# Attention in one block a two pairs of heads instead of two, from the tenth two pairs on

## The chip, the cores and the metric

One core of a Trainium2 chip. The metric is the device time of one execution in microseconds (us); of the kernel before there are three runs, with a median of 1277.4. Engines are named as in the profile: PE is TensorE (PEld its weight loads), DVE VectorE, ACT ScalarE, POOL GpSimd, SP the queue of SyncE, which issues most DMAs.

## The reference, cut to what matters

Eight batch elements, 12 heads, 448 rows, head dimension 64; all in float32.

```python
def rmsnorm(x, g): return x / sqrt(mean(x * x, -1) + 1e-06) * g
scores = 1 / sqrt(64) * rmsnorm(q, g_q) @ rmsnorm(k, g_k).T
attn   = exp(scores - max) / (sum + 1e-09)
x      = (attn @ v), heads side by side                      # (8, 448, 768)
h      = relu(x.T @ w_tok1) @ w_tok2;   u = x + h.T          # token mixing, 256 wide
out    = u + relu(u @ w_ch1) @ w_ch2                         # channel mixing, 1536 wide
```

## The kernel before, in words

**What is computed where.** The kernel works on one batch element's mixing while it computes the attention of the next element between the mixing's matmuls. Heads go in pairs (p, 48 in all, 6 an element), and attention goes in steps of two pairs (t, 24 in all, 3 an element), so that the four heads of a step fill the four 64x64 quarters of TensorE. For key block k of 64 rows (7 of them, `NK`), `score(t, k)` (line 451) does the score matmuls of four heads into two PSUM tiles and two exponentials on ScalarE into an SBUF tile `e`; `values(pair, k)` (521) multiplies `e` with v and accumulates in one PSUM tile `o_ps` a pair; `group_sums` (495) adds the `e` tiles up on VectorE; `row_sums` (540) adds over rows with matmuls of ones into `d_ps`; `denominators` (546) has three kinds of part: `begin` transposes `d_ps` on VectorE and takes the reciprocal, `raw` copies `o_ps` to SBUF on ScalarE, `end` spreads the reciprocal by another transpose and multiplies, both on VectorE. A matmul of float32 stands in the trace as two instructions, so a score step is x8.

**Norms of a later step.** q and k of pairs n and n+1 are loaded by SP (`loads`, 1405, 8 DMAs a pair for pairs from 12 on), squared on ScalarE (`square`, 1432), reduced on VectorE (`reduce`, 1446); then `roots` (1510) gives the parts `fold` (four ScalarE copies), `guess` (VectorE) and three `newton` steps, each of four instructions (GpSimd for pairs from 20 on); `scale` (1501) multiplies on VectorE, and `turn_qk` (423) transposes on VectorE and, for q (i = 0), multiplies by g on ScalarE.

**Mixing of an element b.** `tok1` (843) in halves h = 0 and 1 of the channels (for the second half the rows left over go first, four 64-row matmuls a half, line 854), relu on ScalarE (`tok1_out`); `tok2` (886), six products, each evacuated by VectorE (line 894), and `moving_sums` (902). Then 21 channel units `ch1` (997; 3 groups of seven products, i = 0 to 6, 12 matmul instructions each), of which i = 0 and i = 4 are evacuated by a ScalarE copy (after i = 4 two additions on GpSimd follow), the others by VectorE; then 30 halves of products with w_ch2 (`ch2`, 1065; 15 products f in two halves x, 8 matmul instructions each), whose evacuation is written out in `C_STEPS`, that of f = 0 being a ScalarE copy. Element 1 has 12 halves `plain_2` (1051) instead. All their products use `m_tile`, of which there are two buffers (`ps_M`, line 140); score and d tiles share four (`ps_S`, 138), `o_ps` has two (139). x of an element is transposed from the attention's output by `trans_x` (814) on VectorE, sent to DRAM and loaded again (`send_x`, `load_x`), by SP or, for the second half of element 2, by GpSimd.

**Order.** Every engine but SP runs in the order in which the Python program calls things (`manual_schedule`, line 88). The order is written out by hand: lists of items (cost, function), joined by `merge` (66), which takes from the list that is least far on by its costs, and by `place` (638), which puts blocks at given places among the mixing units and deals the small items that follow a block evenly over the units up to the next block. `run` (170) calls the items, and `later` (162) calls a function when the sum of the costs has passed a time. The `load_units` (925) prefetch keeps up to seven weight units ahead on SP.

**Attention of t = 9 on.** Up to t = 8 attention comes in four `att_step`s (657) a t. From t = `BIG` = 9 on, `big_step` gives two blocks a t. The first block has the scores of key blocks 0 and 1, the last values (key blocks 4, 5 and 6) and row sums of the t before, and score 2; the second has scores 3 and 4, values 0 to 3, scores 5 and 6. The first square of the next pairs is ahead of a first block, the first reduce and second square inside it, the scales and two of the four transposes right after a second block. The first block of t = 9 stands in element 1; elements 2 to 6 have six blocks each, ahead of mixing units 0, 6, 11, 17, 23 and 31 (`BLOCKS`, 1240), counted from the element's first channel unit; the last of element 6 holds only the end of t = 23.

There is a second arm of the program (`shifted`) for inputs of large scale, which these inputs don't take.

Of the kernel before, what the change touches and what calls it, by code (L numbers as in the profile page):

```python
# [83 lines left out]
def whole(ctx, tc, shifted, pre, q, k, v, g_q, g_k, moe_w_tok1, moe_w_tok2, moe_w_ch1, moe_w_ch2, out):  # L84
# [13 lines left out]
    NPAIR = H // 2  # L98
# [15 lines left out]
    NM = S // P  # L114
    assert S - NM * P == D and NM == NS - 1 and NJ == 2

    UNITS = 8
    WCOLS = 512

# [287 lines left out]

    def load_v(p):
        b, hs = heads(p)
        st["v", p] = vt = pre.v_0 if p == 0 else st["v45"][:, p - 4, :] if p in (4, 5) else pre.v_t[p % 3]  # L410
        for a in range(2):
            nc.sync.dma_start(
                out=vt[rows_of(p, a)].rearrange("r (k d) -> r k d", d=D),
                in_=v[b, hs][a].rearrange("(k r) d -> r k d", r=D))
# [36 lines left out]
    def score(t, k):  # L451

        e = st["e", t, k] = e_tile(t >= BIG and ((t - BIG) * NK + k) % 5 == 4)
        pss = [s_tile("s_ps") for i in range(2)]
        for i in range(2):
            qkT = st["qkT", 2 * t + i]
            for a in range(2):
                h = slice(a * D, a * D + D)
                nc.tensor.matmul(  # L459
                    out=pss[i][rows_of(i, a), 0:S], lhsT=qkT[h, 1, k * D:(k + 1) * D], rhs=qkT[h, 0, :],  # L460
                    start=True, stop=True)
        for i in range(2):
            nc.scalar.activation(out=e[:, i, :], in_=pss[i][:, 0:S], func=AF.Exp)  # L463
# [82 lines left out]
    def denominators(ps):  # L546

        def begin(p):
            b, j = divmod(p, NPAIR)
            if j == 0:  # L550
                st["uT", b] = uT_pool.tile([P, NC, S], F32, name="uT")
            ps = st.pop(("d", p))

            dt = rd_pool.tile([P, S], F32, name="dt", tag="rd")
            if shifted:
                nc.vector.tensor_scalar(dt[:], ps[:, 0:S], 1e-9, None, ALU.add)
                src = dt[:]
            else:

                src = ps[:, 0:S]  # L560
            nc.vector.transpose(out=dt[:], in_=src)
            st["rc", p] = rc = pre.nt_pool.tile([P, NB], F32, name="rc")
            nc.vector.reciprocal(out=rc[:], in_=dt[:].rearrange("p (n c) -> p n c", c=32)[:, :, 0])

        def raw(p):

            b, j = divmod(p, NPAIR)
            to = st["uT", b][:, j, :]
            nc.scalar.copy(out=to, in_=st["o", p][:, 0:S])
            st["o", p] = to  # L570

        def end(p):
            b, j = divmod(p, NPAIR)
            rd = rd_pool.tile([P, S], F32, name="rd", tag="rd")
            nc.vector.transpose(
                out=rd[:].rearrange("p (n c) -> p n c", c=32),
                in_=st.pop(("rc", p))[:].unsqueeze(2).to_broadcast([P, NB, 32]))
            nc.vector.tensor_tensor(out=st["uT", b][:, j, :], in0=st.pop(("o", p))[:, 0:S], in1=rd[:], op=ALU.mult)

        parts = [lambda p=p: begin(p) for p in ps]  # L580
        if ps[0] < NPAIR:
# [4 lines left out]
    BIG = NPAIR + NPAIR // 2  # L586

    def big_step(t, second):

        p, n = 2 * t, 2 * t + 2  # L590
        pair, last, live, more = (p, p + 1), (p - 2, p - 1), p < NP, 2 * t + 2 < NP
        item = lambda fn, *a, c=0.4: (c, lambda: fn(*a))
        loads = lambda j: [(0.3, fn) for fn in pre.loads(j, st, nc.sync, nc.sync)] if j < NP else []

        def first_block():
            if live:
                score(t, 0)
                score(t, 1)
# [21 lines left out]
        if not second:  # L620
            squares = [item(fn, i, st) for i in (n, n + 1) for fn in (pre.square, pre.reduce)] if more else []
            ahead, beside = (squares[:1], squares[3:]) if t > BIG else ([], [])
            between = [item(group_sums, t, k) for k in (1, 2) if live]
            ends, roots = ([(0.4, fn) for fn in fns] for fns in (denominators(last), pre.roots(n, st) if more else []))
            if t == BIG:
                return ahead, (5.4, first_block), beside, between + ends + [
                    item(load_v, i, c=0.0) for i in pair] + squares + roots
            between += roots[:1] + ends[:2] + roots[1:2]
            between += [it for both in zip(ends[2:], roots[2:4]) for it in both] if more else ends[2:]
            between += roots[4:] + [item(load_v, i, c=0.0) for i in pair if live]  # L630
            return ahead, (5.4, first_block), beside, between
        beside = [item(scale, n), item(scale, n + 1), item(turn_qk, n, 1), item(turn_qk, n, 0)] if more else []
        beside += [item(group_sums, t, k) for k in (3, 4)]
        between = [item(turn_qk, n + 1, 1), item(turn_qk, n + 1, 0)] + loads(n + 2) if more else []
        between += [item(group_sums, t, k) for k in (5, 6)] + loads(n + 3)
        return [], (6.2, second_block), beside, between

    def place(units, blocks, at):

        res, i, rest = [], 0, []  # L640
        for j, (ahead, block, beside, between) in list(zip(at, blocks)) + [(len(units), ([], None, [], []))]:
            n, done = j - i, 0
            for m in range(n):
                if m == n - 1 and block:
                    res += ahead
                res.append(units[i + m])
                upto = -(-len(rest) * (m + 1) // n)
                res += rest[done:upto]
                done = upto
            if not n:  # L650
                res += rest + ahead
            i, rest = j, between
            if block:
                res += [block] + beside
        return res

    def att_step(g):
# [95 lines left out]
            items.append((0.0, lambda: load_v(p + 1)))  # L753
        if live and s == 1 and 5 < p + 2 < NP:
            items.append((0.0, lambda: load_v(p + 2)))
        js = []
        if live and s == 0:
            js = [n, n + 1] if pre.plain(p) else [n + 1]
# [493 lines left out]
    left, (some, sums) = [], sum_items()  # L1252
    for b in range(B):
        early, double = middle_items(b)
        if b == 0:
# [21 lines left out]
        att = []  # L1277
# [301 lines left out]
```

## Time and profile before

| what | value |
|---|---|
| runs, us | 1277.4, 1273.76, 1279.42 (median 1277.4) |
| profiled execution, us | 1277.84, its span 1275.4 |
| granted TensorE clock, mean | 0.997 |
| score matmuls (line 459, qkT) | x1260, 144.2 us busy |
| value matmuls (line 532, e) | x1148, 129.8 us busy |
| exponentials (line 463, e) | x294, 554 ns each |
| row additions (line 500, es and e) | x90, 1139 ns each |
| normalising multiply (line 1507, 128x896) | x36, 1276 ns each |
| transposes of q and k (line 436) | x72, 618 ns each |

The span runs from the first to the last instruction of the profiled execution; 2.4 us of its time lie around it. The chain of waits starts from the last instruction and goes back at each step to what released it, or to the instruction before it on its engine; its lines give start, length, engine, tile and line. A timeline line gives start, length, engine, line, operation, out<-in with shapes, and in brackets how long the engine had been idle and what released it.

### The profile page before, as it was taken

How to read it: one execution, taken by the hardware profiler on the slowest of the kernel's cores; microseconds unless marked ns; L12 is line 12 of the kernel's file. 1: busy time of each engine (PE TensorE's matmuls, PEld its weight loads, DVE VectorE, ACT ScalarE, POOL GpSimd, SP SyncE). 2: the span in 40 equal slices, each digit the busy share in tenths (PEclk: the TensorE clock that was granted, in tenths of full speed). 3: DMA queues.
4: the chain of work that ended last, by engine and by line, in shares of the span. 5: the costliest groups of instructions: out<-in, count | busy, mean ns of one | idle time of the engine just before them, and what ended most of it. 6: DMA issues, size and time to landing. Idle time of an engine off the chain costs nothing.

```text
span 1275.4 us, 20051 instructions
## 1 busy us (share of the span) xinstructions
PE 1252.2 (98%) x7250; PEld 891.1 (70%) x7250; DVE 796.5 (62%) x1241; ACT 393.9 (31%) x785; POOL 407.0 (32%) x646
## 2 busy tenths in 40 slices
PE   6999999999999999999999999999999999999998
PEld 3444444457645488796778777885787867797998
DVE  6988879756663455855577356765558456554243
ACT  6664433124330134402442044312343024300210
POOL 2310651044994822231223112241122322131222
PEclk9999999999999899999999999999999999999999
DMA  9666687899889686695758767685866864376654
GB/s 204 158 172 174 197 226 188 197 263 253 224 216 260 139 200 162 146 244 110 169 146 188 181 147 181 147 223 121 181 159 150 231 136 139 116 199 145 192 174 105
DMA packets 480272, 228.37 MB, mean 179 GB/s; under 512 B 362900, under 2 KB 440084, under 8 KB 480164
## 3 DMA queue, kind: packets, MB, share of 16 engines
q1 hardware_dynamic: 472626, 211.85, 67.7%
q0 software_dynamic: 4512, 14.46, 3.9%
q8 instruction: 59, 0.97, 0.3%
q10 hardware_dynamic: 3026, 0.69, 0.3%
q14 instruction: 49, 0.40, 0.1%
HBM read 184.26 MB, written 42.66 MB: 178 GB/s over the span
## 4 chain that ended last, share of the span: by engine, by line
PE 88%; DVE 4%; DMA 3%; SPq 1%; ACT 1%; issue 1%; DVEq 0%; ACTq 0%
PE m_ps L1009 26%; PE m_ps L1075 22%; PE s_ps L459 10%; PE o_ps L532 9%; PE m_ps L889 6%; PE m_ps L979 5%; PE m_ps L847 2%; PE t_ps L847 2%; PE m_ps L1058 1%; PE d_ps L512 1%; PE m_ps L512 1%; DMA raw<-wp 1%; DVE stage L383 1%; PE m_ps L854 1%; PE t_ps L433 1%
## 5 line engine op out<-in xcount | busy, mean ns | idle before, releaser
L1075 PE MATMUL m_ps<-hb,unit 128*128 128x224 f32 x1440 | 277.2, 354 | 0.0
L1075 PEld LDWEIGHTS m_ps<-hb,unit 128*128 128x128 f32 x1440 | 270.9, 190 | 8.8 <-issue 7.7
L1009 PE MATMUL m_ps<-tu,unit 128*128 128x224 f32 x1008 | 201.6, 355 | 1.3 <-ACT r L1019 1.3
L1009 PEld LDWEIGHTS m_ps<-tu,unit 128*128 128x128 f32 x1008 | 189.1, 190 | 15.0 <-issue 9.2
L463 ACT ACTIVATE e<-s_ps 128x448 f32<-128x448 f32 x294 | 138.6, 554 | 177.5 <-PE s_ps L459 168.9
L1009 PE MATMUL m_ps<-uT,unit 128*128 128x224 f32 x756 | 151.2, 354 | 0.8 <-DVE hb L1015 0.8
L1009 PEld LDWEIGHTS m_ps<-uT,unit 128*128 128x128 f32 x756 | 142.2, 190 | 7.9 <-issue 4.6
L459 PE MATMUL s_ps<-qkT 64*64 64x448 f32 x1260 | 144.2, 545 | 0.8 <-ACT x L829 0.8
L532 PE MATMUL o_ps<-e,v 64*64 64x448 f32 x1148 | 129.8, 538 | 0.0
L500 DVE TENSOR_TENSOR es<-es,e 128x896 f32<-128x896 f32 x90 | 102.5, 1139 | 13.4 <-ACT e L463 8.4
L1015 DVE TENSOR_TENSOR hb<-m_ps,r 128x448 f32<-128x448 f32 x63 | 39.1, 621 | 106.2 <-POOL r L1015 57.4
L1015 POOL TENSOR_TENSOR hb<-r,r 128x448 f32<-128x448 f32 x21 | 23.9, 1140 | 239.0 <-ACT r L1031 239.0
L459 PEld LDWEIGHTS s_ps<-qkT 64*64 64x64 f32 x1260 | 45.5, 132 | 69.5 <-issue 59.2
L532 PEld LDWEIGHTS o_ps<-e,v 64*64 64x64 f32 x1148 | 45.9, 133 | 61.9 <-issue 59.6
L1486 POOL TENSOR_TENSOR nt<-rs 128x56 f32<-128x56 f32 (+1 forms) x54 | 21.8, 403 | 201.4 <-DVE rs L1478 198.5
L1016 ACT ACTIVATE hb<-hb 128x448 f32<-128x448 f32 x84 | 48.4, 577 | 100.4 <-DVE hb L1015 77.4
L1090 POOL TENSOR_TENSOR uT<-uT,r 128x448 f32<-128x448 f32 x42 | 51.4, 1241 | 78.3 <-DVE r L1090 46.6
L889 PE MATMUL m_ps<-w_sb,h 128*128 128x448 f32 x192 | 75.2, 544 | 0.3 <-DVE uT L894 0.3
L324 POOL TENSOR_TENSOR raw<-raw 128x128 f32<-128x128 f32 x128 | 64.8, 527 | 21.8 <-DMA raw<-wp 17.3
L894 DVE TENSOR_TENSOR uT<-uT,m_ps 128x448 f32<-128x448 f32 x48 | 29.3, 614 | 65.9 <-PE m_ps L889 65.8
L1456 DVE TENSOR_REDUCE ms<-sq 128x28 f32<-128x896 f32 (+2 forms) x44 | 47.4, 1080 | 36.7 <-ACT sq L1443 29.6
L1015 DVE TENSOR_TENSOR r<-m_ps,r 128x448 f32<-128x448 f32 x42 | 26.1, 622 | 64.5 <-PE m_ps L1009 64.5
(153 smaller groups left out, 1626.9 us busy)
## 6 DMA issues: line engine op xcount, KB each, us to landing
unit<-ws SPq DMA_DIRECT2D x267, 384.0 KB, 4.2
raw<-in_moe_w_ch_dram SPq DMA_DIRECT2D x72, 256.0 KB, 3.5
v<-in_v_dram SPq DMA_DIRECT2D x96, 112.0 KB, 3.5
out_dram<-turned SPq DMA_DIRECT2D x182, 56.0 KB, 2.0
xs<-xt SPq DMA_DIRECT2D x52, 168.0 KB, 4.8
qk_t<-in_q_dram SPq DMA_DIRECT2D x144, 56.0 KB, 3.5
qk_t<-in_k_dram SPq DMA_DIRECT2D x144, 56.0 KB, 3.9
x<-xs SPq DMA_DIRECT2D x39, 192.0 KB, 4.0
```

The lines of the kernel that those rows point to most:

```text
L324: nc.gpsimd.tensor_tensor(out=at[o], in0=at[x], in1=at[y], op=ALU.add if op == "+" else ALU.subtract)
L459: nc.tensor.matmul(out=pss[i][rows_of(i, a), 0:S], lhsT=qkT[h, 1, k * D:(k + 1) * D], rhs=qkT[h, 0, :], start=True, stop=True)
L463: nc.scalar.activation(out=e[:, i, :], in_=pss[i][:, 0:S], func=AF.Exp)
L500: nc.vector.tensor_tensor(out=es[:], in0=(es if k > 1 else st["e", t, 0])[:], in1=st["e", t, k][:], op=ALU.add)
L532: nc.tensor.matmul(out=st["o", p][a * D:(a + 1) * D, 0:S], lhsT=vt[rows, k * D:(k + 1) * D], rhs=e[rows, :], **kw)
L847: nc.tensor.matmul(out=st["t1", h][jc][:, 0:HC], lhsT=w1_sb[:, c, jc * P:(jc + 1) * P], rhs=st["x", b, h][:, :, c, :], start=start and c = ...
L889: nc.tensor.matmul(out=ps[:, 0:S], lhsT=st["h1", jc][:, cc * P:(cc + 1) * P], rhs=w2_sb[:, jc].rearrange("p c r -> p (c r)"), start=(jc == ...
L979: nc.tensor.matmul(out=ps, lhsT=a[:, o + 2 * half, :], rhs=natural(half * KF + t) if wide else u[:, half * KC + t, :], start=(t == 0 and h ...
L1009: nc.tensor.matmul(out=ps[:, j * HS:(j + 1) * HS], lhsT=w[:, t, j, :], rhs=m, start=(t == 0), stop=(t == KC - 1))
L1015: add = lambda e, o, x, y: e.tensor_tensor(out=o, in0=x, in1=y, op=ALU.add)
L1075: nc.tensor.matmul(out=ps[:, x * HS:(x + 1) * HS], lhsT=st["w"][:, tile_at % 6, :], rhs=hb[:, X_SLOT[f], i, :], start=(i == 0), stop=(i == 3))
L1090: e.tensor_tensor(out=get(out), in0=get(x_), in1=get(y), op=ALU.add if op == "+" else ALU.subtract)
```

## The change

From t = 9 on, attention comes in one block a t. It holds scores 0 and 1 of t, values 5 and 6 and the row sums of the t before, then for that t `begin` and `raw` of both pairs (so `o_ps` is copied to SBUF by ScalarE, which was done for the first element only), then score 2, and from there value k-3, row addition k-1 and score k in turn for k = 3 to 6, and value 4. The last row addition follows the block. Elements 2 to 6 have three blocks each, ahead of mixing units 2, 15 and 31.

What follows a block is dealt out by `place` alone, in one row: the two `end`s, the v loads of the next t, the norms (two squares, two reduces, five root parts), the scales, transposes and loads; nothing of it is ahead of a block or inside one any more. After an element's third block only `end`s, v loads and the first two norm items stand; the rest of the norms (`behind`) is merged with the last mixing units and the second half of x, and the scales, transposes and loads (`carry`) are dealt over the next element's units from its `tok1` up to its first block. The whole norms of t = 10, which stood behind the block of t = 9 in element 1, go with that carry into element 2. The v tiles of pairs from 18 on use four buffers instead of three, and pair 19's load is moved to t = 8. In element 1, the list of attention items that `merge` joins with the mixing changes its costs: 5.4 for the first block and 6.0 for what follows it before, 11.3 and 1.2 after.

```diff
+    BIG = NPAIR + NPAIR // 2
...
     def load_v(p):
         b, hs = heads(p)
-        st["v", p] = vt = pre.v_0 if p == 0 else st["v45"][:, p - 4, :] if p in (4, 5) else pre.v_t[p % 3]
+        if p >= 2 * BIG and not shifted:
+            vt = (pre.v_0, pre.v_t[0])[p % 2] if p // 2 % 2 else pre.v_t[1 + p % 2]
+        else:
+            vt = pre.v_0 if p == 0 else st["v45"][:, p - 4, :] if p in (4, 5) else pre.v_t[p % 3]
+        st["v", p] = vt
...
-        if ps[0] < NPAIR:
+        if ps[0] < NPAIR or ps[0] >= 2 * BIG - 2 and not shifted:
             parts += [lambda p=p: raw(p) for p in ps]
...
-    def big_step(t, second):
+    def big_step(t):
...
+        ends = denominators(last)
-        def first_block():
+        def block():
             if live:
                 score(t, 0)
                 score(t, 1)
-            if more and t > BIG:
-                pre.reduce(n, st)
-                pre.square(n + 1, st)
-            for k in range(NK - 2 - (t > BIG), NK):
+            for k in (NK - 2, NK - 1):
                 values(last, k)
             row_sums(t - 1)
             for i in last:
                 st.pop(("v", i))
-            if live:
-                score(t, 2)
-
-        def second_block():
-            score(t, 3)
-            score(t, 4)
-            for k in range(4):
-                values(pair, k)
-            score(t, 5)
-            score(t, 6)
+            for part in ends[:4]:
+                part()
+            if not live:
+                return
+            group_sums(t, 1)
+            score(t, 2)
+            for k in range(3, NK):
+                values(pair, k - 3)
+                group_sums(t, k - 1)
+                score(t, k)
+            values(pair, NK - 3)
...
+        beside = [item(group_sums, t, NK - 1)] if live else []
+        ends_ = [(0.4, fn) for fn in ends[4:]]
+        if not more:
+            return (11.3 if live else 2.3, block), beside, ends_, [], []
+        norms = [item(fn, i, st) for i in (n, n + 1) for fn in (pre.square, pre.reduce)]
+        norms += [(0.4, fn) for fn in pre.roots(n, st)]
+        turned = [item(scale, n), item(scale, n + 1), item(turn_qk, n, 1), item(turn_qk, n, 0)] + loads(n + 2)
+        turned += [item(turn_qk, n + 1, 1), item(turn_qk, n + 1, 0)] + loads(n + 3)
+        values_in = [item(load_v, i, c=0.0) for i in (n, n + 1)]
+        return (11.3, block), beside, ends_ + values_in, norms, turned
...
-    BLOCKS = (0, 6, 11, 17, 23, 31)
+    BLOCKS = (2, 15, 31)
...
-                ahead, block, beside, between = big_step(BIG, False)
-                att = att[6:] + att_items(lo + 10, lo + per - 1) + ahead + [block] + beside + between
+                block, beside, ends_, norms, turned = big_step(BIG)
+                att = att[6:] + att_items(lo + 10, lo + per - 1) + [block] + beside + ends_
+                carry = norms + turned
         elif b + AHEAD < B:
             t = (b + AHEAD) * NPAIR // 2
-            blocks = [big_step(t + i // 2, i % 2) for i in range(1, NPAIR + 1)]
-            blocks[4][3].extend(x_items(b + 1, 0))
-            early = place(early, blocks, [near(early, at) for at in BLOCKS])
+            steps = [big_step(t + i) for i in range(1, NPAIR // 2 + 1)]
+            blocks = [(block, beside, ends_ + norms + turned) for block, beside, ends_, norms, turned in steps[:2]]
+            blocks[1][2].extend(x_items(b + 1, 0))
+            block, beside, ends_, norms, turned = steps[2]
+            blocks.append((block, beside, ends_ + norms[:2]))
+            early = place(early, blocks, [near(early, at) for at in BLOCKS], carry)
+            behind, carry = norms[2:], turned
...
-                last = merge(last, x_items(b + 1, 1))
+                last = merge(last, x_items(b + 1, 1) + behind)
```

More of the change, by code (lines that the diff above doesn't have):

```diff
@@ L585, in whole @@
     NG = 2 * NP
-    BIG = NPAIR + NPAIR // 2
-    def big_step(t, second):
+    assert BIG % 2
+    def big_step(t):
         p, n = 2 * t, 2 * t + 2
@@ L617, in second_block @@
+            values(pair, NK - 3)
             for i in pair:
                 st.pop(("qkT", i))
[L620 to L641, printed above, removed]
+        beside = [item(group_sums, t, NK - 1)] if live else []
@@ L642, in place @@
+        return (11.3, block), beside, ends_ + values_in, norms, turned
+    def place(units, blocks, at, rest):
+        res, i = [], 0
+        for j, (block, beside, between) in list(zip(at, blocks)) + [(len(units), (None, [], []))]:
             n, done = j - i, 0
             for m in range(n):
-                if m == n - 1 and block:
-                    res += ahead
                 res.append(units[i + m])
@@ L650, in place @@
             if not n:
-                res += rest + ahead
+                res += rest
             i, rest = j, between
@@ L755, in att_step @@
             items.append((0.0, lambda: load_v(p + 2)))
+            if t == BIG - 1 and not shifted:
+                items.append((0.0, lambda: load_v(p + 3)))
         js = []
@@ L1251, in whole @@
         att_items(0, 8) + merge(att_items(8, AHEAD * per + 1), x_items(0, 0)), weight_items(0, BEFORE)))
-    left, (some, sums) = [], sum_items()
+    left, carry, (some, sums) = [], [], sum_items()
     for b in range(B):
@@ L1276, in whole @@
         lo = (b + AHEAD) * per + 1
-        att = []
+        att, behind = [], []
         if b + AHEAD < B and (shifted or b < 2):
```

## The prediction

> **What bounds the kernel now.** I read the page first, then the chain of waits by stretches, then the engines' timelines where the chain leaves TensorE. The page:
>
> ```profile
> PE 1252.2 (98%) x7250; PEld 891.1 (70%) x7250; DVE 796.5 (62%) x1241; ACT 393.9 (31%) x785; POOL 407.0 (32%) x646
> PE 88%; DVE 4%; DMA 3%; SPq 1%; ACT 1%; issue 1%; DVEq 0%; ACTq 0%
> ```
>
> TensorE is busy nearly throughout and is 88% of the chain that ended last. The chain of waits from 440 us on (start, us, what) holds nothing but TensorE up to the last microseconds:
>
> ```profile
> 439.55 1.67 PE s_ps L459 x16
> 441.22 3.01 PE o_ps L532 x32
> 444.22 1.50 PE s_ps L459 x16
> 445.73 13.82 PE m_ps L1009 x72
> 459.54 1.66 PE s_ps L459 x16
> ...
> 502.12 9.28 PE m_ps L1009 x48
> ```
>
> So after 440 us no VectorE, ScalarE or DMA work costs anything; what can be saved is TensorE's own time, and any new wait is lost in full. Two prices are in these lines. Sixteen score matmuls take 1.50 inside a block but 1.67 at its start: 0.17 to enter. Channel matmuls: (13.82 - 9.28) / (72 - 48) = 0.189 each, and 72 x 0.189 = 13.62, so each stretch carries 0.20 for leaving a block. **A block costs 0.37 us** beyond its matmuls.
>
> Before 440 the chain has two holes. At the start of element 2, x comes late:
>
> ```profile
> 416.18 4.96 DMA x<-xs
> 421.14 0.14 issue
> 421.27 2.31 PE t_ps L854 x4
> 423.58 6.85 PE t_ps L847 x12
> ```
>
> The same two rows at the start of element 3:
>
> ```profile
> 573.79 0.65 PE t_ps L854 x4
> 574.44 4.07 PE t_ps L847 x12
> ```
>
> TensorE idled 2 us for x, then worked at about half speed for 8 us (the windows view grants 0.52 of the clock from 422 to 429). Against its matmuls' usual spacing, this hole costs 5.9. The other, at 328 to 332, is VectorE and ScalarE evacuating late while they normalise pairs 16 and 17:
>
> ```profile
> 323.85 2.53 DVE qk_t L1507 x2
> ...
> 328.07 0.56 ACT hb L1016
> ...
> 331.86 2.54 PE m_ps L1009 x12
> ```
>
> It costs 2.7 (TensorE's gaps in loading weights there are 1.2 and 1.65).
>
> The normalisation of the next two pairs, which the change moves, is a chain over four engines (timeline, 394 to 403; the last two lines from 589):
>
> ```profile
> 394.66 0.95 ACT L1443 ACTIVATE sq<-qk_t 128x896 f32<-128x896 f32 x1 [12.16 <-DMA qk_t<-in_k_dram]
> 395.64 1.09 DVE L1456 TENSOR_REDUCE ms<-sq 128x28 f32<-128x896 f32 x1 [6.87 <-ACT sq L1443]
> 396.76 1.01 ACT L1464 COPY half<-ms 32x56 f32<-32x56 f32 x4 [1.15 <-DVE ms L1456]
> ...
> 398.34 0.27 POOL L1486 TENSOR_TENSOR nt<-rs 128x56 f32<-128x56 f32 x1 [6.78 <-DVE rs L1478]
> ...
> 402.31 0.30 POOL L1489 TENSOR_TENSOR rs<-nt,rs 128x56 f32<-128x56 f32 x1
> ...
> 589.27 2.55 DVE L1507 TENSOR_TENSOR qk_t<-qk_t,rs 128x896 f32<-128x896 f32 x2
> 591.75 1.16 DVE L436 STREAM_TRANSPOSE qkT<-qk_t 128x448 f32<-128x448 f32 x2
> ```
>
> Second square to roots ready: 402.6 - 394.66 = **8.0**, of which GpSimd's three steps are 4.2. Then VectorE scales (2.55) and transposes (1.16).
>
> [...]
>
> **The change, part by part.** The sum is against the profiled execution, 1277.84 (span 1275.4).
>
> 1. **Fewer blocks.** Before: one block in element 1 and six in each of elements 2 to 6, 31. After: 16. Scores, values and row sums stay the same matmuls. 15 x 0.37 = **-5.5**; nothing hides it.
>
> 2. **Inside a block.** A score step, a value step and a row sum take 0.75 each on TensorE. Counting from the block's start, the row sums end at 0.17 + 5 x 0.75 = 3.92; the fourth score is due at 5.42 and needs their two PSUM tiles, which VectorE's two transposes free at 3.92 + 0.07 + 1.43 = 5.42 (1.43: two transposes with a reciprocal between, 541.10 to 542.53). The first values, due at 4.67, need the two new ScalarE copies (0.5 each, from 3.24): 4.3. Exponentials take 0.96 per 1.5 of TensorE. So it just fits; I take 16 x 0.06 = **+1.0** (0 to +5 if VectorE is behind when it enters). Row additions end 1.2 after the block, before the next unit's evacuation at 2.3.
>
> 3. **First gap of elements 2 to 5** (13 units, 35 items, dealt by `place`). From the block's end, a channel unit is 12 x 0.189 = 2.27. The second square is dealt after the unit with i = 4 (third in the gap), so on ScalarE it stands behind that unit's copy, which ends at 6.81 + 0.1 + 0.53 = 7.44. Chain 8.0: roots at 15.45. The unit with i = 0 (sixth in the gap) is followed on VectorE by scale, transpose, transpose: VectorE is bound till 15.45 + 2.55 + 1.16 = 19.2, and only then evacuates the seventh unit (0.6): 19.8. The ninth unit needs that PSUM buffer (two of them) at 8 x 2.27 = 18.16. Wait 1.65. Element 6 has no loads to deal, its items lie further apart, no wait. 4 x 1.65 = **+6.6** (0 to +10).
>
> 4. **Second gap of elements 2 to 5** (16 units, 38 items). GpSimd takes the Newton steps after the adds of the i = 4 unit: its end 9.08, copy 9.7, two adds (1.14 each) 12.05, Newton 16.3, scale 18.85, transposes 20.0, ScalarE's multiply (0.67) 20.7, and behind that, on ScalarE, the copy of the first w_ch2 product, 21.25. The third product needs its buffer at 6 x 2.27 + 4 x 1.51 = 19.67. Wait 1.6. 4 x 1.6 = **+6.4** (0 to +10).
>
> 5. **Third block.** Two norm items follow it, the rest goes among the last units, far from a due evacuation: 0. x's second half is transposed earlier: 0, its wait is hidden already. In elements 3 to 6 the carried scales are done before tok2, but the last two transposes (1.2) fall between the tok2 evacuations; the first channel unit, which used to have a block ahead of it, waits 0.45: 4 x 0.45 = **+1.8** (0 to +4).
>
> 6. **Start of element 2.** It inherits the whole norms of pairs 20 and 21. Count from the first 64-row matmul of tok1's second half, X (572.95 in element 3). The first square stands behind the relu at X + 4.15; square 0.95, reduce 1.1, a y transpose 0.65, reduce 1.1, fold 1.05, guess 0.4: X + 9.4. VectorE evacuates the first tok2 product after the guess, at X + 10.0; the third needed it at X + 8.55. GpSimd's 4.2 end at X + 13.6, scale X + 15, second product evacuated X + 15.65; the fourth was due at X + 11.55. Scale, moving sums (1.1), two transposes, a y transpose, evacuation: X + 20.5; the fifth was due at X + 17.15. Waits 1.45 + 4.1 + 3.35 = 8.9. An idle of 4.1 will halve the clock as the 2 us did, about 3; formed weights on GpSimd may add 0.7. **+12.6** (+6 to +17). On the other side x should now be in time: TensorE reaches it 7.0 later (nine more steps of 0.75 and the switch), x's last transpose moves from 400.4 to about 405.3, so x lands near 424 to 426 and is needed at 426: **-5.9** (-5.9 to 0).
>
> 7. **Element 1.** The attention list's total grows by 1.1 in 94, and its merge puts two attention steps one unit earlier. VectorE's scales then no longer stand together ahead of the evacuation at 327: **-2.6** (-2.7 to +2).
>
> Loads, values and their queue: SP has 16 loads of about 0.5 to issue per step, with a block of 11.4 and several units before they are read. At nothing; cover gone, a late load would hold ScalarE at the square.
>
> **Sum:** -5.5 + 1.0 + 6.6 + 6.4 + 1.8 + 12.6 - 5.9 - 2.6 = **+14.4**: 1292.2; on the median of the runs, 1277.4, 1291.8. I say **1292**.
>
> **Rivals.**
> - *Drains and x only* (faster): the chains of 3, 4 and 6 have slack I don't see, and part 6 keeps only its gain: 1277.8 - 5.5 - 5.9 - 2.6 + 1 = 1265. For it: the waits of 3 and 4 are only 1.6 after chains of 20. Against: those chains are sums of measured durations in strict order. It decides where the chain is under 6.4 rather than 8.0 long. 0.18.
> - *Only element 2's start stalls*: 1277.8 - 5.5 - 2.6 + 1 + 1.8 + 6.7 = 1279. 0.17.
> - *The clock drops at the 1.6 us waits too*: each of eight then costs up to 4 more: 1300 to 1324. Against: the 1.65 gap at 331 was followed by full speed. 0.07.
>
> My own case has 0.58, and alone would reach from 1284 to 1300. A difference within 0.5% (6.4 us) can't be told from none here. Faster 0.18 (the first rival), within 0.5% 0.18 (the second and the foot of mine), slower 0.64. The range runs from the first rival's upper part to 1304.
>
> **What would show it.** The chain should hold 16 blocks from 390 us on, each 11.4 long without a break; evacuations waited for after seven units of the first gap and at the third w_ch2 product; VectorE waiting for GpSimd's roots (L1489's group) just before; holes of about 1.5, 4 and 3.4 in the tok2 stage of element 2; no wait for x. If tok2 of element 2 runs without holes, part 6 is wrong; if the chain is all TensorE again, the first rival is right.

## The result, and the profile after

The kernel after takes 1305.88 us (median of 6 runs, 1302.78 to 1308.79), the kernel before 1276.32 in the same session (6 runs): the ratio is 1.0238, with a 95% interval from 1.0214 to 1.0261. The forecast was 1292.0, with a range from 1268 to 1304. The direction was right; the loss is twice as large (+29.6 against +14.4). The profiled execution of after took 1302.78, with a span of 1301.0; it is the fastest of the six.

Three rows of the page of after: busy time of the engines, the chain that ended last by engine, and the group of the second channel matmul (busy and mean ns, then TensorE's idle time ahead of it).

```profile
PE 1258.3 (97%) x7250; PEld 920.7 (71%) x7250; DVE 795.9 (61%) x1241; ACT 412.2 (32%) x817; POOL 404.1 (31%) x646
PE 81%; DVE 7%; DMA 3%; POOL 2%; ACT 2%; issue 2%; SPq 2%; DVEq 0%; ACTq 0%; POOLq 0%
L1073 PE MATMUL m_ps<-hb,unit 128*128 128x224 f32 x1440 | 282.5, 359 | 9.9 <-ACT r L1084 9.9
```

TensorE has the same 7250 matmuls, but its share of the chain fell from 88% to 81%: other engines now stand in it. Where they stand shows in the chain of waits of after from 425 us on (start, us, what):

```profile
425.45 0.85 PE m_ps L852 x4
426.30 0.65 PE t_ps L852 x4
...
447.34 3.27 PE m_ps L887 x8
...
455.26 1.66 PE s_ps L464 x16
...
460.69 0.98 PE s_ps L464 x8
...
466.93 13.83 PE m_ps L1007 x72
480.78 2.68 DMA unit<-ws
...
484.47 1.16 DVE qkT L441 x2
485.64 0.52 DVE hb L1013
...
486.20 11.62 PE m_ps L1007 x60
...
525.61 2.89 DMA unit<-ws
528.50 0.93 DVE qk_t L1510
...
529.50 1.18 DVE qkT L441 x2
530.70 0.67 ACT qkT L444
531.37 0.43 ACT r L1084
...
531.84 11.02 PE m_ps L1073 x48
```

Five things are in it. The 64-row matmuls at 426 need no DMA any more: x is in time. Between 426.30 and 447.34, left out here, nearly every row is the norm chain of pairs 20 and 21. The block, from 455.26 on, is unbroken, but its fourth score row takes 0.98 and not 0.75. And the chain leaves TensorE after 72 matmuls of the first gap and again at the third product of w_ch2 in the second. The row "DMA unit<-ws" there is no cause: a weight load merely ended last by the profile. The timeline names GpSimd's roots (below), and in an experiment the scale comes earlier when only the roots do.

**Where the 26 us are.** For each stretch of one kind I took the time from its start to the next stretch's start, less its matmul instructions times their usual spacing (0.189 for channel matmuls, 0.376 for tok2, 0.0938 inside a block). So the second gap's w_ch2 stretch, 523.14 to 542.79 with 80 instructions, has 19.65 - 15.14 = 4.5 of excess. From 240 us to the end, before has 29.3 of it and after 55.4; the difference of 26.1 is close to that of the spans, 25.6. (What the medians differ by beyond that, some 4 us, isn't explained by one pair of traces.) A wait, in what follows, is the length of a single gap over that spacing.

| place | before | after | difference | predicted |
|---|---|---|---|---|
| 1. switches, 31 and 16 blocks | 11.5 | 5.9 | -5.6 | -5.5 |
| 2. inside blocks | 0 | 15 x 0.25 | +3.8 | +1.0 |
| 3. first gap, elements 2 to 5 | 0 | 4 x 1.1 | +4.5 | +6.6 |
| 4. second gap, elements 2 to 5 | 0 | 4 x 4.4 | +17.7 | +6.4 |
| 5. tok2, elements 3 to 6 | 0.2 each | 0.35 each | +0.6 | +1.8 |
| 6. element 2: tok2; x | 0.2; 5.9 | 10.6; 0 | +10.4; -5.9 | +12.6; -5.9 |
| 7. element 1, stall | 2.9 | 2.4 | -0.4 | -2.6 |
| element 6, block of t = 23 | 0 | 1.3 | +1.3 | "no wait" |

The table adds up to +26.4. One row is less firm than it looks: in the three runs further below whose edits leave element 2's tok2 alone, its excess is 12.2 to 12.8 and not 10.6, because the clock stays at half for 10.2 us there and not for 6.8. Two thirds of the sum is the second gap, whose timeline in after is this (start, us, engine, line, operation; in brackets how long the engine idled and what released it):

```profile
518.18 0.95 ACT L1446 ACTIVATE sq<-qk_t 128x896 f32<-128x896 f32 x1 [4.12 <-DVE ms L1459]
...
520.72 1.14 POOL L1013 TENSOR_TENSOR r<-r,r 128x448 f32<-128x448 f32 x1
...
521.31 0.62 DVE L1476 SCALAR_TENSOR_TENSOR ms<-ms,half 128x56 f32<-128x56 f32 x1 [1.05 <-ACT half L1467]
...
522.60 1.25 POOL L1490 TENSOR_TENSOR nt<-nt,ms 128x56 f32<-128x56 f32 x1
522.61 1.08 DVE L1047 TENSOR_TENSOR hb<-hb 128x896 f32<-128x896 f32 x1
...
527.49 2.10 DVE L1510 TENSOR_TENSOR qk_t<-qk_t,rs 128x896 f32<-128x896 f32 x2 [3.26 <-POOL rs L1492]
...
531.84 11.02 PE L1073 MATMUL m_ps<-hb,unit 128*128 128x224 f32 x48 [2.48 <-ACT r L1084]
```

The scale waits 3.26 for GpSimd, and at the end of what follows it TensorE waits 2.64. Two small operations are far too long: L1476 takes 0.62 where it takes 0.22 alone, until GpSimd's addition is over (521.86); L1490 takes 1.25 and not 0.30, until VectorE's L1047 is over (523.69). Then the clock: two windows of after, with busy time of PE, PEld, DVE, ACT and POOL (instructions), PEclk, DMA share, GB/s.

```profile
523.00:531.00 8.00, 6.36 (x34) 6.01 (x32) 4.74 (x7) 1.18 (x3) 3.63 (x11) 1.00 0.37 117
531.00:540.00 9.00, 8.16 (x34) 7.84 (x35) 5.49 (x8) 1.53 (x4) 3.21 (x2) 0.81 0.75 152
```

After the wait, TensorE has 0.81 of the clock over 9 us, 1.7 lost: the wait of 2.64 became 4.4.

### The profile page after: what moved, and what is told of

It is laid out like the page before. It is cut to its first block, busy times and chain, and to the rows that moved or that the text cites. A ratio compares the mean times of both kernels' runs of the same rounds, so it can differ in the third digit from the quotient of the medians.

```text
span 1301.0 us, 20148 instructions
## 1 busy us (share of the span) xinstructions
PE 1258.3 (97%) x7250; PEld 920.7 (71%) x7250; DVE 795.9 (61%) x1241; ACT 412.2 (32%) x817; POOL 404.1 (31%) x646
## 4 chain that ended last, share of the span: by engine, by line
PE 81%; DVE 7%; DMA 3%; POOL 2%; ACT 2%; issue 2%; SPq 2%; DVEq 0%; ACTq 0%; POOLq 0%
PE m_ps L1007 20%; PE m_ps L1073 20%; PE s_ps L464 9%; PE o_ps L537 9%; PE m_ps L977 5%; PE m_ps L1056 4%; PE m_ps L887 4%; PE m_ps L845 3%; DMA unit<-ws 2%; PE t_ps L845 2%; DVE qkT L441 2%; PE d_ps L517 1%; PE m_ps L517 1%; SPq L1420 1%; POOL raw L325 1%
## 5 line engine op out<-in xcount | busy, mean ns | idle before, releaser
L1073 PE MATMUL m_ps<-hb,unit 128*128 128x224 f32 x1440 | 282.5, 359 | 9.9 <-ACT r L1084 9.9
L1073 PEld LDWEIGHTS m_ps<-hb,unit 128*128 128x128 f32 x1440 | 277.1, 194 | 16.2 <-ACT r L1084 11.3
L464 PE MATMUL s_ps<-qkT 64*64 64x448 f32 x1260 | 166.0, 544 | 1.3 <-ACT x L827 0.8
L537 PE MATMUL o_ps<-e,v 64*64 64x448 f32 x972 | 141.3, 538 | 0.0
L1013 POOL TENSOR_TENSOR hb<-r,r 128x448 f32<-128x448 f32 x21 | 24.9, 1187 | 301.9 <-ACT r L1029 301.9
L464 PEld LDWEIGHTS s_ps<-qkT 64*64 64x64 f32 x1260 | 59.9, 132 | 64.4 <-issue 41.0
L1013 DVE TENSOR_TENSOR hb<-m_ps,r 128x448 f32<-128x448 f32 x63 | 39.1, 620 | 91.4 <-PE m_ps L1007 45.6
L537 PEld LDWEIGHTS o_ps<-e,v 64*64 64x64 f32 x972 | 49.9, 133 | 45.0 <-issue 31.9
L325 POOL TENSOR_TENSOR raw<-raw 128x128 f32<-128x128 f32 x128 | 68.6, 555 | 21.6 <-DMA raw<-wp 17.1
L887 PEld LDWEIGHTS m_ps<-w_sb,h 128*128 128x128 f32 x192 | 35.8, 193 | 46.7 <-issue 26.7
L444 ACT ACTIVATE qkT<-qkT,g_t 128x448 f32<-128x448 f32 x36 | 24.1, 669 | 138.3 <-DVE qkT L441 138.1
L1510 DVE TENSOR_TENSOR qk_t<-qk_t,rs 128x896 f32<-128x896 f32 (+1 forms) x42 | 47.0, 1155 | 32.5 <-POOL rs L1492 32.4
```

The costliest lines, as they stand in the source:

```text
L325: nc.gpsimd.tensor_tensor(out=at[o], in0=at[x], in1=at[y], op=ALU.add if op == "+" else ALU.subtract)
L464: nc.tensor.matmul(out=pss[i][rows_of(i, a), 0:S], lhsT=qkT[h, 1, k * D:(k + 1) * D], rhs=qkT[h, 0, :], start=True, stop=True)
L537: nc.tensor.matmul(out=st["o", p][a * D:(a + 1) * D, 0:S], lhsT=vt[rows, k * D:(k + 1) * D], rhs=e[rows, :], **kw)
L887: nc.tensor.matmul(out=ps[:, 0:S], lhsT=st["h1", jc][:, cc * P:(cc + 1) * P], rhs=w2_sb[:, jc].rearrange("p c r -> p (c r)"), start=(jc == ...
L1013: add = lambda e, o, x, y: e.tensor_tensor(out=o, in0=x, in1=y, op=ALU.add)
L1073: nc.tensor.matmul(out=ps[:, x * HS:(x + 1) * HS], lhsT=st["w"][:, tile_at % 6, :], rhs=hb[:, X_SLOT[f], i, :], start=(i == 0), stop=(i == 3))
```

## The experiments

**Theory**: every loss of more than 1 us comes from one chain, squares to roots to scale to transposes, that a gap now holds whole, so that evacuations stand in VectorE's and ScalarE's queues behind its waits; the place where the chain crosses GpSimd is what makes it late. **Rivals**: VectorE's queue is simply too full, or the chain is as long as it is wherever it is dealt; for element 2, x comes late again once the wait that hides it is gone. All ratios are against the kernel before in the same session; after has 1.0238. The sessions' medians of before are 1273.93 (first four kernels), 1274.88 (next three) and 1274.38 (last two).

### The first norms back in element 1

```diff
-                att = att[6:] + att_items(lo + 10, lo + per - 1) + [block] + beside + ends_
-                carry = norms + turned
+                att = att[6:] + att_items(lo + 10, lo + per - 1) + [block] + beside + ends_ + norms
+                carry = turned
```

> Only the norms of pairs 20 and 21 go back behind the block of t = 9 in element 1; the rest is the changed kernel. Chain theory (norms stand in strict order ahead of evacuations): the tok2 stage of element 2 loses its 10.5 us of waits and halved clock and comes out near 9.4 for its 24 matmuls; the second half of x may come late again, as it did before the change, which would give back up to 6. So 1295 to 1300 against 1306 for the changed kernel. Rival (the long block itself is the loss): no change, 1304 or more. The waits in the first gaps (1.1 each) and at the third w_ch2 product (2.6 each) stay in both.

Measured: 1290.93 (4 runs), ratio 1.0131 (1.0103 to 1.0160). Its chain of waits at the start of element 2:

```profile
425.89 0.65 PE t_ps L852 x4
426.54 4.07 PE t_ps L845 x12
430.61 6.03 PE m_ps L887 x16
```

Sixteen tok2 matmuls run in one piece where after had waits of 1.9, 5.7 and 1.5; the excess of that tok2 stretch is 0.33, from 10.6. And the four 64-row matmuls take 0.65: x is in time without that wait. So step 6 holds in both halves, and the x gain belongs to the rest of the change and not to the delay. This run also shows the clock apart from the wait. In elements 2 to 5 TensorE waits 2.63 to 2.65 in the second gap, but the excess is 2.8 in elements 2 and 4 and 4.5 in 3 and 5. The windows after that wait, in elements 2 and 3:

```profile
521.00:529.00 8.00, 7.84 (x41) 7.84 (x42) 4.86 (x7) 1.31 (x3) 3.22 (x2) 1.00 0.75 152
672.00:680.00 8.00, 7.36 (x30) 6.99 (x31) 5.29 (x8) 1.25 (x3) 3.21 (x2) 0.79 0.78 156
```

The same wait is followed by full clock once and by 0.79 the other time: 1.7 us is the price of the drop alone. Elements 3 and 4 of this trace stand side by side in the last section.

### Both transposes of the row sums ahead of both reciprocals

```diff
-        parts = [lambda p=p: begin(p) for p in ps]
+        parts = [lambda p=p: begin(p) for p in ps] + [lambda p=p: inverse(p) for p in ps] * apart
...
-            for part in ends[:4]:
+            for part in ends[:6]:
```

(`begin` then only transposes, `inverse` takes the reciprocal.)

> Inside each block both transposes of the row sums come before both reciprocals. If the fourth score waits for the second transpose, its wait of 0.25 a block falls to about 0.02: blocks of 120 matmuls take 11.45 instead of 11.69, 15 x 0.24 = 3.6 less, about 1302. If ScalarE's copies of the values hold it up instead, nothing changes.

Measured: 1299.56 (4 runs), ratio 1.0198 (1.0168 to 1.0227). The excess of a block falls from 0.42 to 0.18 in 14 of the 15, 14 x 0.24 = 3.4 (that of t = 23 keeps its 1.7; its first scores wait for another reason, given below). So the fourth score waits for the second transpose, and for nothing else. In the traces, two clock drops fewer in the second gaps (after waits of 2.65 to 2.67, two of four) give another 3.4, tok2 of element 2 takes 1.9 more, and element 1's stall 0.8 less; none of these three lies where the edit is.

### Norms ahead of the last block's divisions

```diff
-            blocks = [(block, beside, ends_ + norms + turned) for block, beside, ends_, norms, turned in steps[:2]]
+            blocks = [(block, beside, norms[:4] + ends_ + norms[4:] + turned)
+                      for block, beside, ends_, norms, turned in steps[:2]]
```

> In the first and second gaps the squares and reduces are dealt ahead of the denominators' last parts, so the chain of the norms starts some 4 us earlier. If it is the chain's own length that decides, both waits vanish: 4 x (1.1 + 4.4) = 22 less, about 1284. If, as worked out, the Newton steps are held behind GpSimd's additions after the unit with i = 4 whatever comes before, the first gap keeps its 1.1 and the second gap loses only what the late second square cost there, about 0.9 of 2.6: 1296 to 1303.

Measured: 1300.29 (4 runs), ratio 1.0196 (1.0166 to 1.0227). The squares are done earlier, yet the first gap's wait is 1.26 where it was 1.08: the guess there stands on VectorE behind an evacuation that waits for GpSimd's two additions for the fifth product (they end at 480.01), so the roots are as late as before. In the second gap the wait is 2.04; that was followed by a halved clock in elements 4 and 5 (excess 3.9) and not in 2 and 3 (2.2). An earlier start of the chain alone is worth little; what stands ahead of it on GpSimd decides.

### Six empty items ahead of the scales, second gap

```diff
+            idle = [(0.0, lambda: None)]
+            blocks = [(block, beside, ends_ + norms + idle * more + turned)
+                      for more, (block, beside, ends_, norms, turned) in zip((0, 6), steps)]
```

> Six empty items between norms and scales in the second gap of each element alone, so that the scales and transposes are called after the first w_ch2 product's evacuation instead of before it; no work is changed. Chain theory: the wait of 2.6 at the third w_ch2 product and the halved clock after it go, 4 x 4.4 = 17.7 less, about 1288, and the 80 matmuls after the second gap's channel units take 15.2 instead of 19.65. Rival (the engines are simply short of time in that gap, wherever the items stand): the wait moves to a later product, over 1300. Rival (the clock drops because of the long block, not the wait): 1.9 of the 4.4 stay, about 1296.

Measured: 1297.39 (4 runs), ratio 1.0177 (1.0147 to 1.0206): 9 above the theory's 1288. The time is near the 1296 of the second rival, but the trace isn't: the clock stays whole in all four second gaps, with the long blocks as they were. The w_ch2 stretch falls from 4.5 to 1.1, but the ch1 stretch ahead of it gets 1.0 that it didn't have, and tok2 of element 2 takes 2.2 more (the half clock again). The timeline shows why (element 3):

```profile
673.97 0.99 ACT L1469 COPY half<-ms 32x56 f32<-32x56 f32 x4 [1.15 <-DVE ms L1461]
674.99 0.53 ACT L1029 COPY r<-m_ps 128x448 f32<-128x448 f32 x1
...
675.57 2.54 PE L1007 MATMUL m_ps<-tu,unit 128*128 128x224 f32 x12 [0.27 <-ACT r L1029]
...
678.53 1.05 POOL L1493 TENSOR_SCALAR nt<-nt 128x56 f32<-128x56 f32 x1
```

Dealing 44 items over 16 units instead of 38 moved the four fold copies ahead of the copy of the fifth product, and so TensorE, GpSimd's additions and the roots came later. Room that is made by packing other items closer isn't free.

### Newton steps on VectorE

```diff
-        if 2 < p < 2 * self.NPAIR or p >= self.far:
+        if 2 < p < 2 * self.NPAIR:
```

> The nine small Newton steps of pairs 20 and up go from GpSimd to VectorE (three operations a step, 0.32 us each in element 1's rows, 2.9 in all), nothing else is changed against the kernel after. Theory (the scales, and behind them the evacuations, wait for roots that GpSimd delivers late): in the second gap the guess is done at 522.2, nine steps and the two evacuations between them end near 525.7 in place of 527.45, so TensorE's wait falls from 2.6 to about 0.9 and the clock isn't halved: 4.4 becomes 0.9, four times, -14. First gap: the wait of 1.1 goes, -4.4. Start of element 2: 10.6 becomes about 6.5, -4. Together about 1283. Rival (VectorE's queue itself is what is late, and 2.9 us more in it ahead of each gap's evacuations cost what GpSimd's hand-over cost): gaps as before, the first gap's wait over 1, time 1298 or more.

Measured: 1290.82 (4 runs), ratio 1.0110 (1.0084 to 1.0136), about midway between 1283 and 1298, so the time alone decides nothing; the trace does. The first gap runs without a wait; its row in the chain of waits is one piece, where after had two:

```profile
468.26 29.71 PE m_ps L1007 x156
```

The second gap, in the timeline:

```profile
525.90 0.22 DVE L1501 TENSOR_TENSOR nt<-nt,ms 128x56 f32<-128x56 f32 x1
...
526.52 2.10 DVE L1510 TENSOR_TENSOR qk_t<-qk_t,rs 128x896 f32<-128x896 f32 x2 [0.16 <-DMA unit<-ws]
528.54 1.16 DVE L441 STREAM_TRANSPOSE qkT<-qk_t 128x448 f32<-128x448 f32 x2
...
529.74 0.67 ACT L444 ACTIVATE qkT<-qkT,g_t 128x448 f32<-128x448 f32 x1 [3.38 <-DVE qkT L441]
530.31 0.51 ACT L1084 COPY r<-m_ps 128x448 f32<-128x448 f32 x1
530.87 2.35 PE L1073 MATMUL m_ps<-hb,unit 128*128 128x224 f32 x11 [1.37 <-ACT r L1084]
```

The scale no longer waits for roots, so GpSimd was the cause and VectorE has the room in these two gaps: the first theory, against the full queue. The clock stays whole after a wait of 1.5, and the excess is 1.7 in place of 4.5. What remains is order alone: scales, transposes and ScalarE's multiplication stand ahead of the copy of the first w_ch2 product. Two things fell short: tok2 of element 2 still has 8.6, where I had hoped for 6.5; and the third stretch of each element gets 1.0 (its cause is shown further below).

### A tile for each of the two squares

The squares of a step share one tile, so the second square waits for the first reduction (the 4.12 above). Here they are kept as bfloat16 in its two halves, a coarser rounding of the squares.

```diff
-            sq = self.sq[:].rearrange("p r d -> p (r d)")[:, 0:n * d].rearrange("p (r d) -> p r d", d=d)
+            sq = self.sq[:].rearrange("p r d -> p (r d)").bitcast(mybir.dt.bfloat16)
+            sq = sq[:, p % 2 * n * d:(p % 2 + 1) * n * d].rearrange("p (r d) -> p r d", d=d)
```

> The squares of the two pairs of a step are kept as bfloat16 in the two halves of the one tile (a coarser rounding of the squares, nothing else), so the second square doesn't wait for the first reduction. Theory A (the shared tile sets the chain of the second gap): the roots come 1.1 earlier, the wait of 2.6 becomes 1.5, the clock drop may go: 4 x (1.1 to 2.9), 1294 to 1301. Theory B (GpSimd can't begin before its two adds for the fifth product are done, at 521.86, which is only 0.4 before it began): the wait falls by 0.4 at most, time within 2 of the kernel after unless the clock drop goes as well (then up to 7 less).

Measured: 1297.27 (4 runs), ratio 1.0161 (1.0134 to 1.0188). A square and a reduction take as long as in after (0.95 and 1.08), so only the wait between them is gone. The wait is 1.99 in place of 2.64, and in all four elements the clock stays whole (excess 2.2). Theory A wanted 1.5. The timeline shows where the rest of its 1.1 went:

```profile
525.44 1.13 POOL L1013 TENSOR_TENSOR r<-r,r 128x448 f32<-128x448 f32 x1
...
525.59 1.03 DVE L1482 TENSOR_SCALAR rs<-ms 128x56 int32<-128x56 int32 x1
...
526.70 0.28 POOL L1490 TENSOR_TENSOR nt<-rs 128x56 f32<-128x56 f32 x1
```

The guess comes earlier, but runs into GpSimd's second addition and lasts until that is over: 1.03 for 0.19. So GpSimd's additions hold the roots, as B said; the shared tile is worth 0.65 of wait, more than B's 0.4.

### All remedies together, and what was left

The next kernel joins the first norms in element 1, the parted transposes and the Newton steps on VectorE, and pads the transposes of element 6, which has no loads to deal:

```diff
-            blocks = [(block, beside, ends_ + norms + turned) for block, beside, ends_, norms, turned in steps[:2]]
+            idle = [(0.0, lambda: None)]
+            blocks = [(block, beside, ends_ + norms + turned + idle * (22 - len(turned)))
+                      for block, beside, ends_, norms, turned in steps[:2]]
```

> All remedies together against the kernel after: Newton steps on VectorE, the first norms of the new order (pairs 20 and 21) back in element 1, both transposes of the row sums ahead of both reciprocals in the block, and, where no loads are left to deal (element 6), sixteen empty items behind the transposes, so that they don't stand right before the next block. Theory: of the excess over the kernel before (+26) go tok2 of element 2 (-10.5), the block's inside (-3.8), the first gap (-4.4), the second gap from 4.4 to 0.9 (-14), the last step of element 6 (-1.3); what stays is -5.6 for the switches, -5.9 for x and +4.6: 1269 to 1273, below the kernel before. Rival (VectorE's queue is full: the nine steps make waits of their own in each gap): 1280 or more.

Measured: 1278.09 (20 runs), ratio 1.0026 (1.0016 to 1.0037): 5 short of the theory. Tok2 of element 2, the blocks, the first gap and element 6 are as expected; the second gap keeps 1.7 where 0.9 was expected, and the stretch behind the third block has 1.25 in place of 0.1. The timeline there:

```profile
551.30 2.22 POOL L1094 TENSOR_TENSOR uT<-uT,r 128x448 f32<-128x448 f32 x2 [0.61 <-DVE r L1094]
...
552.54 1.03 DVE L1489 TENSOR_SCALAR rs<-ms 128x56 int32<-128x56 int32 x1
553.47 2.09 POOL L1053 TENSOR_TENSOR hb<-hb 128x896 f32<-128x896 f32 x1
553.60 2.04 DVE L1508 SCALAR_TENSOR_TENSOR nt<-rs 128x56 f32<-128x56 f32 x1
...
556.72 15.40 PE L1079 MATMUL m_ps<-hb,unit 128*128 128x224 f32 x80 [0.90 <-DVE uT L1094]
```

Two VectorE operations of about 0.2 take 1.03 and 2.04, each until the GpSimd operation beside it ends (553.52, 555.56); an evacuation stands behind them.

So the roots behind the third block go back to GpSimd:

```diff
-        if 2 < p < 2 * self.NPAIR:
+        if 2 < p < 2 * self.NPAIR or p >= self.far and p % self.NPAIR == 2:
```

> As the run with all remedies together, but the Newton steps of the pairs that are normalised behind an element's third block stay on GpSimd; only those of the first two gaps go to VectorE. In the run before, small VectorE operations of that third stretch took 1.03 and 2.04 in place of 0.2, each ending with a GpSimd operation beside it, and TensorE then waited 0.9 to 1.0. Theory (the two engines hold each other up, and GpSimd's own chain has the time there): the excess of the third stretch falls from 1.25 to 0.1, four times, -4.6: about 1273.5. Rival (VectorE is late there for another reason, its transposes and additions): 1277 or more.

Measured: 1273.91 (20 runs), ratio 0.9998 (0.9988 to 1.0007); that stretch is at 0.1. At last the order in the second gap, with nothing packed closer ahead of it (`two` joins two items):

```diff
+                if len(turned) == 22:
+                    at = 22 - 2 * more
+                    turned = turned[:2] + idle * more + turned[2:at] + [
+                        two(*turned[i:i + 2]) for i in range(at, 22, 2)]
```

(`more` is 0 in the first gap and 4 in the second.)

> As the run named mixed, and in the second gap four empty items stand between the two scales and the transposes of the normalised pair (its last eight loads are dealt two at a time, so that the rest stays where it is). Theory: TensorE's last wait of 1.4 in this gap is for ScalarE's copy of the first product of the second channel matmul, which stands on ScalarE behind the multiplication of the transposed pair; with the transposes dealt over a unit later it goes: another -6, about 1267.5, 0.5% below the kernel before. Rival (the copy or the additions are late for VectorE's scales alone): the wait stays over 1, 1272 or more.

Measured: 1267.81 (6 runs), ratio 0.9945 (0.9928 to 0.9962), the only kernel here that is clearly below the one before. Its chain by engine, and rows of its chain of waits:

```profile
PE 89%; DVE 5%; SPq 2%; DMA 1%; issue 1%; ACT 1%; DVEq 0%; ACTq 0%
```

```profile
433.54 6.03 PE m_ps L893 x16
...
458.97 29.71 PE m_ps L1013 x156
...
500.11 13.82 PE m_ps L1013 x72
```

From element 2's first block on it is all TensorE again. An element (3 to 5) takes 146.9 where before takes 147.9: three blocks' switches in place of six.

## Why the prediction was right and wrong

**1, switches: right.** -5.6 against -5.5; the last kernel keeps it whole.

**2, inside the block: mis-sized.** The fourth score waits for the two transposes, as worked out. "3.92 + 0.07" was the failed term. It puts the row sums' end where the next matmul starts, in the trace of after at 381.86; but the transpose starts 0.24 later:

```profile
382.10 0.65 DVE L566 STREAM_TRANSPOSE dt<-d_ps 128x448 f32<-128x448 f32 x1 [7.83 <-PE d_ps L517]
```

The row sums' matmuls come at a spacing of 0.094, but each takes 0.54 in the profile, so that the last ends at 382.04, 0.06 ahead of the transpose. The fit that was "just" is short by this tail: 0.25 a block, which the order in the second experiment takes away.

**3, first gap: right mechanism**, 1.1 a time for 1.65. On VectorE the seventh unit's evacuation (L1013, 485.56) stands behind two scales that begin at 482.46, after a wait of 3.32 for the roots. The two scales take 2.09 with GpSimd idle beside them where I used 2.55.

**4, second gap: the step that failed**, 11 of the 12 us by which the sum fell short. TensorE's own time was right (the third product due at 19.67, measured 19.8). The chain's was short. "Adds 12.05, Newton 16.3" is in truth 12.4 and 18.0, counted from 509.42: the fifth product's copy ends 0.4 late, in part because the second square, held up by the shared tile, stands ahead of it on ScalarE; the fold and the guess come late, L1476 beside GpSimd's addition (+0.4 before the first Newton step); and a Newton step runs into VectorE's L1047 (+0.95). The faster scales give 0.5 back. That makes a wait of 2.64 for 1.6. And then the price of such a wait: I took its length for its cost, while the clock dropped after 2.64 and added 1.7. The rival "the clock drops at the 1.6 us waits too" (0.07) named the range in which the time fell, 1300 to 1324, though not the place: it dropped at one of the two waits, because that was longer than I thought, and never after the first gap's 1.1. That the other rows together miss by only 0.7 is luck: rows 3, 5 and 6 were 5.5 too high, rows 2, 7 and element 6 were 6.3 too low.

In three places the traces show a small operation of VectorE or GpSimd that lasts until about when a longer one of the other engine is over, as closely as the profile's GpSimd spans allow: in after VectorE's L1476 took 0.62 for 0.22 beside GpSimd's L1013, and GpSimd's L1490 1.25 for 0.30 beside VectorE's L1047; in the run that joined all remedies VectorE's L1508 took 2.04 for about 0.2 beside GpSimd's L1053. Why, the runs don't show. I priced both engines' rows as if each ran alone.

**5, tok2 tails: there, but smaller**, +0.6 for +1.8.

**6, element 2: right in both halves**, +10.4 for +12.6 and -5.9 for -5.9; the first experiment shows each by itself. The waits add up to 9.1 for 8.9. The clock took less than the 3 that I gave it, since TensorE stood idle for more than half of the 6.8 us at half clock (busy 3.35 of the 6.83 from 439.69 in after).

**7, element 1: wrong**, -0.4 for -2.6. The trace of after shows GpSimd forming weights from 313.61 to 320.83 (line 325), having waited 17 for their load; its additions for the fifth product, and VectorE's evacuation behind them, come only then. (In before the first of these additions starts at 317.64, in after at 320.80.) This was read from the traces and not tested, and the size isn't firm: in the runs whose edits leave element 1 alone the same stretch has 1.6, 2.5, 3.0 and 4.2 of excess for after's 2.4.

**Missed: element 6.** "Its items lie further apart, no wait" looked at the gap's middle. Without loads behind them the last transposes stand right ahead of the next block, whose scores wait 1.0 for them. With the padding, in the run that joined all remedies, it is gone.

The rival on the faster side, "drains and x only" at 1265 (its drains stand for the 0.37 us that a block costs beyond its matmuls), describes no run of the change itself. The last kernel, with all of the chain's waits mended, comes half of the way: 6.6 below before in its session, where the rival had 12.8.

## What to carry to other kernels

A chain that crosses engines can be moved into one gap only if its end has room ahead of the next evacuation in the same queue; add up the chain with each engine's other work in it, and deal the waiting step late rather than its predecessors early. Price small VectorE and GpSimd operations at up to the length of the operation that the other engine may be in (here about 0.2 became up to 2.04). Where a wait comes out like those of the second gap (of twenty with 1.98 to 2.67 us, ten were followed by half clock), write down the clock drop, 1.7 us here, as a second price, one that may or may not be due, and let the range reach it.

## What the hardware showed unexpectedly

- **Waits of one length, 2.64 us, were followed by half clock or by full clock, and the two differ in how the wait lies on a grid of 3.413 us.** Waits of 2.63 to 2.67 in the second gap were followed by half clock in four of four elements of after, but in two of four in each of the first two experiments; waits of 2.04 in two of four. Waits of 1.99 (four, the two halves) and of 1.5 (twelve, in the three kernels with Newton steps on VectorE and this gap's order unchanged) were never followed by it. In the traces of before and after all changes of the granted clock lie on a grid of 3.413 us, to within 0.002; where the grid lies relative to the kernel's start differs between the two (a change at 422.32 in before, at 439.69 in after: 5.09 steps apart). Two steps of such a grid with a wait of 2.64 in the first experiment, elements 3 and 4, the first with the step after it (length, then busy time of the engines and PEclk as above):

```profile
670.40:673.82 3.42, 1.18 (x6) 1.18 (x7) 2.04 (x3) 1.09 (x2) 1.13 (x1) 1.00 0.38 61
673.82:677.23 3.41, 3.41 (x11) 3.05 (x10) 2.70 (x4) 0.66 (x1) 1.64 (x1) 0.50 0.79 167
...
824.00:827.41 3.41, 1.58 (x8) 1.58 (x9) 2.02 (x4) 1.09 (x2) 1.13 (x1) 1.00 0.43 71
```

  In element 3, 2.24 of the wait fall into one step, and the next has half clock; in element 4 only 1.83, the rest lies in the step before, and the next step has full clock. It is so in all twenty second gaps with waits of 1.98 to 2.67 (elements 2 to 5 of five traces): the ten with 2.04 or more in one step (in after 2.48, 2.48, 2.49 and 2.08) were followed by half clock, the ten with 1.99 or less were not. So a wait of 2.64 was dear or cheap by where it happened to fall. A drop there lasted one step, 3.41 us with 0.50 of the clock, and cost 1.7. The two numbers are no bound: at the late x of before the clock fell for 6.83 us at 422.32, after a step that held only 1.38 of TensorE's idle time, amid 64-row matmuls.
- **One kernel's second gap gained 2.3 us from a wait only 0.65 shorter** (the two halves): 0.65 was the wait itself, the other 1.7 the drop, which did not follow it in any of the four elements.
